# A routed mixture of experts on one core: the next expert's transposes go inside the prepared sequences, and the common tile gets its own PSUM bank

## The chip, the cores and the metric

The kernel runs on one core of a Trainium2 chip. The metric is the device time of one execution in microseconds (us); lower is better. Three runs of the kernel before gave 756.47, 759.58 and 760.03 us, so its median is 759.58 us.

## What is computed

Two blocks follow each other. The first is an attention over 4 batches x 8 heads x 768 positions x 64 columns, in which a position sees the 8 first keys and a window of 96. Its output, as 3072 rows of 512 numbers, goes into a block of 8 experts; each row goes through exactly one of them, the one with the highest cosine similarity. Everything is float32.

```python
expert_idx = np.argmax(logits, axis=1)
gate_w = probs[np.arange(N), expert_idx]
for e in range(E):
    mask = expert_idx == e
    h = np.maximum(x[mask] @ w1[e], 0.0)              # 512 -> 1024
    out[mask] = gate_w[mask, None] * (h @ w2[e])      # 1024 -> 512
```

How many rows an expert gets is known only when the program runs.

## The kernel before

**Attention.** It comes first, writes the 3072 rows to `x_dram`, and writes for each row a slot in `meta` (row number and gate) that is sorted by expert. The change leaves this part as it is.

**Experts.** The eight experts run one after the other, in Python's order of the loop `for e in range(n.E)` (line 840). On TensorE, ScalarE, VectorE and GpSimd the order of the instructions is the order in which the code is written (`manual_schedule`, line 836). Each expert has these steps:

- `load_rows` (line 629): SyncE loads 512 slots of `meta` into `emt`, VectorE casts the row numbers into `ids`, and GpSimd issues four indirect DMAs that gather 4 x 128 rows of `x_dram` into four tiles `xg`. It is written one expert ahead: expert e+1's rows are gathered at the start of expert e.
- `load_weights` (line 133): two DMAs of 2 MB each, into one of two sets of buffers in turn.
- `turn_rows` (line 651): the four tiles `xg` are transposed on TensorE, each with four transposes into one PSUM bank from the pool `work` (L657); VectorE copies each bank into `xT` (L658). In the tables below these are the "transposes" and the "copies".
- the first product (L690): 64 matmuls of `w1` with `xT`, only as wide as the expert has rows, rounded up to a multiple of 32. ScalarE puts the result through a relu into `hT` (L692), GpSimd clears what is left of the last 128 columns (L694).
- the second product, `second` (line 662): for each 128 rows a tile of 16 matmuls with `w2` into a bank of `work` (L668), VectorE multiplies it with the gate into `y` (L671), and GpSimd scatters `y` to the output with an indirect DMA (L672).

**Prepared sequences.** Because the width is known only at run time, the program holds 13 versions ("arms") of an expert's first product and of the tiles j = 1, 2, 3 of its second product, for the widths 128, 160, ... 512. Each engine jumps into the arm that fits (`tc.Switch`, line 682) and at its end jumps to the common code behind all arms. The common code of expert e holds a hint for the next jump (`switch_hint`, line 833), the transposes and copies of expert e+1 (`turn`, called as `between`, line 698), and the tile j = 0 of expert e's second product, which every width needs. The pool `work` has four banks for all of these, and `big` has two buffers of two banks for the first product.

In this data the eight experts take the widths 416, 320, 512, 320, 352, 384, 480 and 384. An arm of width 320, 352 or 384 has two tiles of the second product (j = 1, 2), one of 416, 480 or 512 has three. "The join" below is the stretch from the last matmul in an arm to the first matmul of the next expert's arm; there are seven of them.

Of the kernel before, what the change touches and what calls it, by code (L numbers as in the profile page):

```python
# [9 lines left out]
F32 = mybir.dt.float32  # L10
# [4 lines left out]
PSUM = bass.MemoryType.PSUM  # L15
# [3 lines left out]
P = 128  # L19
NEG = 1e9  # L20
CAP = 512
# [626 lines left out]
    return mt, ids, xgs  # L648


def turn_rows(k, rows):

    xT = k.xtp.tile([P, k.NC, CAP], F32, name="xT", tag="xT")
    for j, xg in enumerate(rows[2]):
        ps = k.work.tile([P, k.NC, P], F32, name="work", tag="work")
        for c in range(k.NC):
            k.nc.tensor.transpose(ps[:, c, :], xg[:, c * P : (c + 1) * P], k.ident[:])  # L657
        k.nc.vector.tensor_copy(out=xT[:, :, j * P : (j + 1) * P], in_=ps[:])  # L658
    return xT


def second(k, rows, hT, w2, j):

    nc = k.nc
    mt, ids, _ = rows
    ps = k.work.tile([P, k.DM], F32, name="work", tag="work")
    for f in range(k.NF):
        nc.tensor.matmul(ps[:], lhsT=hT[:, f, j * P : (j + 1) * P], rhs=w2[:, f, :],  # L668
                         start=f == 0, stop=f == k.NF - 1)
    y = k.yp.tile([P, k.DM], F32, name="y", tag="y")  # L670
    nc.vector.tensor_scalar_mul(y[:], ps[:], mt[:, j, 1:2])  # L671
    nc.gpsimd.indirect_dma_start(  # L672
        out=k.out[:, :], out_offset=bass.IndirectOffsetOnAxis(ap=ids[:, j : j + 1], axis=0),
        in_=y[:], in_offset=None, bounds_check=k.N - 1, oob_is_err=False,
    )


def expert(k, rows, xT, w1, w2, width=None, between=None):

    nc, tc = k.nc, k.tc  # L680
    hT = k.hp.tile([P, k.NF, CAP], F32, name="hT", tag="hT")
    arms = [len(WIDTHS) - 1] if width is None else tc.Switch(width.index, len(WIDTHS), hint=width.hint)
    for arm in arms:
        w = WIDTHS[arm]
        for f2 in range(k.NF // 2):
# [6 lines left out]
            nc.scalar.activation(hT[:, 2 * f2 : 2 * f2 + 2, 0:w], ps[:, :, 0:w], AF.Relu)  # L692
            if w % P:
                nc.gpsimd.memset(hT[:, 2 * f2 : 2 * f2 + 2, w : -(-w // P) * P], 0.0)  # L694
        for j in range(1, -(-w // P)):
            second(k, rows, hT, w2, j)
    if between:
        between()
    second(k, rows, hT, w2, 0)


# [18 lines left out]
def leftover(k):  # L720
# [18 lines left out]
    with tc.If(any_ > 0):  # L739
# [7 lines left out]
        with ExitStack() as inner:  # L747
# [10 lines left out]
            with tc.For_i(0, E * passes, 1) as i:  # L758
# [3 lines left out]
                with tc.If(n > 0):  # L762
# [2 lines left out]
                    nc.sync.dma_start(w1[:], k.w1[bass.ds(e, 1)].rearrange("o (c p) f -> p (o c) f", p=P))  # L765
                    nc.sync.dma_start(w2[:], k.w2[bass.ds(e, 1)].rearrange("o (f p) m -> p (o f) m", p=P))
                    rows = load_rows(k, k.meta[bass.ds(e * k.N + j * CAP, CAP), :])
                    expert(k, rows, turn_rows(k, rows), w1, w2)


def expert_pools(k, ctx):
# [8 lines left out]
def kernel(  # L780
# [13 lines left out]
    n = Net()  # L794
# [21 lines left out]
    with ExitStack() as moe:  # L816
# [2 lines left out]
        with ExitStack() as inner:  # L819
            window_attention(n, inner)  # L820

        n.work = ctx.enter_context(tc.tile_pool(name="work", bufs=4, space=PSUM))
        n.big = ctx.enter_context(tc.tile_pool(name="big", bufs=2, space=PSUM))
        wp_b = moe.enter_context(tc.tile_pool(name="wp_b", bufs=1))
        expert_pools(n, moe)
        choose_widths(n)
        next_ = Net()

        def prepare(e):
            next_.rows = load_rows(n, n.meta[e * n.N : e * n.N + CAP, :])  # L830

        def turn(e):
            tc.switch_hint(n.widths[e].index, len(WIDTHS), n.widths[e].hint)
            next_.xT = turn_rows(n, next_.rows)

        with tc.manual_schedule(engines=set(ARMS)):
            prepare(0)
            turn(0)
            w = n.w[0]
            for e in range(n.E):  # L840
                now, next_ = next_, Net()
                now.w = w
                if e + 1 < n.E:
                    prepare(e + 1)
                    w = new_weights(n, (wp_a, wp_b)[(e + 1) % 2])
                    load_weights(n, e + 1, w)
                expert(n, now.rows, now.xT, *now.w, n.widths[e], (lambda: turn(e + 1)) if e + 1 < n.E else None)
    n.scatters = None
    leftover(n)

# [27 lines left out]
```

## Time and profile before

| what | value |
|---|---|
| median of three runs | 759.58 us (756.47 to 760.03) |
| the profiled execution's own time | 746.06 us |
| span of the profiled execution | 744.3 us |
| TensorE busy | 629.3 us, 85% of the span |
| VectorE, ScalarE, GpSimd busy | 24%, 19%, 15% |
| attention, to the first matmul of the experts | about 0 to 284.8 us |
| experts, to the last matmul | 284.8 to 728.7 us |

The profile comes from one execution. Its page gives the busy time of each engine, a picture of the span in 40 slices, and the chain of work that ended last. The trace behind it gives each instruction with the idle time before it and what ended that idle time (`<-`). PE is TensorE's matmul side, DVE is VectorE, POOL is GpSimd, SPq is the DMA queue of SyncE. [...] "issue" is idle time in which an engine waited for nothing that the trace shows.

### The profile page before, as it was taken

How to read it: one execution, taken by the hardware profiler on the slowest of the kernel's cores; microseconds unless marked ns; L12 is line 12 of the kernel's file. 1: busy time of each engine (PE TensorE's matmuls, PEld its weight loads, DVE VectorE, ACT ScalarE, POOL GpSimd, SP SyncE). 2: the span in 40 equal slices, each digit the busy share in tenths (PEclk: the TensorE clock that was granted, in tenths of full speed). 3: DMA queues.
4: the chain of work that ended last, by engine and by line, in shares of the span. 5: the costliest groups of instructions: out<-in, count | busy, mean ns of one | idle time of the engine just before them, and what ended most of it. 6: DMA issues, size and time to landing. Idle time of an engine off the chain costs nothing.

```text
span 744.3 us, 8702 instructions
## 1 busy us (share of the span) xinstructions
PE 629.3 (85%) x3314; PEld 347.4 (47%) x3314; DVE 179.3 (24%) x509; ACT 141.0 (19%) x280; POOL 111.2 (15%) x146
## 2 busy tenths in 40 slices
PE   4889989989999408978969997979969969997991
PEld 2556655556566304534634443634535534443540
DVE  2434563564467511011020002011020020011000
ACT  3444543544453200100100100100100100100100
POOL 3110013013003232011112010211112012010010
PEclk9999999998899657997988998997988989997997
DMA  9856676840012942022434103532334134000000
GB/s 223 196 125 185 164 229 56 154 116 15 30 44 26 234 85 88 2 89 101 145 137 140 46 30 130 186 118 82 127 138 143 47 142 177 11 30 14 16 29 20
DMA packets 102683, 75.67 MB, mean 102 GB/s; under 512 B 83440, under 2 KB 83568, under 8 KB 102522
## 3 DMA queue, kind: packets, MB, share of 16 engines
q1 hardware_dynamic: 93610, 58.44, 29.5%
q0 software_dynamic: 5488, 14.71, 5.4%
q8 instruction: 51, 0.84, 0.5%
q10 hardware_dynamic: 3424, 0.79, 0.5%
q14 instruction: 110, 0.90, 0.4%
HBM read 61.11 MB, written 13.59 MB: 100 GB/s over the span
## 4 chain that ended last, share of the span: by engine, by line
PE 77%; DMA 7%; DVE 6%; issue 4%; ACT 2%; POOL 1%; DVEq 1%; another core or an unknown queue 0%; SPq 0%; ACTq 0%; POOLq 0%
PE work L668 27%; PE big L690 23%; PE sp L340 7%; PE od L370 6%; PE tp L323 3%; PE od L376 3%; PE work L657 3%; DMA x_dram<-xs 3%; DVE xT L658 3%; DVE ex L350 1%; DMA w2t<-in_moe_w_dram 1%; PE tp L433 1%; PE tp L408 1%; PE tp L411 1%; DMA meta<-mt,slot 1%
## 5 line engine op out<-in xcount | busy, mean ns | idle before, releaser
L668 PE MATMUL work<-w2t,hT 128*128 128x512 f32 x432 | 203.3, 631 | 5.5 <-DVE xT L658 5.5
L690 PE MATMUL big<-xT,w1t 128*128 128x320 f32 (+5 forms) x512 | 173.9, 501 | 0.9 <-DVE ids L639 0.9
L668 PEld LDWEIGHTS work<-w2t,hT 128*128 128x128 f32 x432 | 87.1, 204 | 115.8 <-issue 106.4
L690 PEld LDWEIGHTS big<-xT,w1t 128*128 128x128 f32 x512 | 98.3, 192 | 76.5 <-issue 42.4
L671 DVE TENSOR_SCALAR y<-work,emt 128x512 f32<-128x512 f32 x27 | 20.3, 751 | 360.8 <-PE work L668 360.8
L692 ACT ACTIVATE hT<-big 128x640 f32<-128x640 f32 (+5 forms) x32 | 26.6, 830 | 422.9 <-PE big L690 422.9
L350 DVE TENSOR_TENSOR ex<-ex,table 126x384 f32<-126x384 f32 (+1 forms) x128 | 67.4, 564 | 82.4 <-ACT ex L344 81.2
L672 POOL DMA_INDIRECT out_dram<-y,ids x27 | 26.8, 993 | 372.9 <-DVE y L671 240.8
L657 PE MATMUL work<-ident,xg 128*128 128x128 f32 x128 | 30.8, 386 | 57.7 <-DVE xT L658 38.3
L340 PE MATMUL sp<-qT,kT 64*126 64x192 f32 (+1 forms) x512 | 67.4, 366 | 6.1 <-ACT qT L328 5.1
L370 PE MATMUL od<-ex,v 126*64 126x192 f32 (+1 forms) x576 | 61.8, 322 | 5.3 <-POOL mt L200 3.8
L344 ACT ACTIVATE ex<-sp 126x768 f32<-126x768 f32 x64 | 49.1, 767 | 75.7 <-PE sp L340 68.2
L340 PEld LDWEIGHTS sp<-qT,kT 64*126 64x126 f32 x512 | 44.0, 197 | 26.7 <-issue 15.5
L657 PEld LDWEIGHTS work<-ident,xg 128*128 128x128 f32 x128 | 20.5, 193 | 69.6 <-DVE xT L658 45.2
L370 PEld LDWEIGHTS od<-ex,v 126*64 126x64 f32 x576 | 34.4, 140 | 24.3 <-issue 13.6
L376 PE MATMUL od<-ex,ones 126*32 126x192 f32 (+1 forms) x576 | 36.2, 321 | 0.0
L658 DVE COPY xT<-work 128x512 f32<-128x512 f32 x32 | 22.1, 692 | 51.7 <-PE work L657 32.0
L643 POOL DMA_INDIRECT xg<-x_dram,ids x32 | 30.9, 966 | 22.7 <-DVE ids L639 13.6
L202 POOL DMA_INDIRECT meta<-mt,slot x24 | 24.4, 1019 | 39.1 <-DVE slot L193 20.6
L323 PE MATMUL tp<-ident,k 128*128 128x128 f32 x96 | 19.9, 330 | 5.7 <-DMA k<-in_k_dram 5.5
L314 POOL COPY v<-v 30x1792 f32<-30x1792 f32 x8 | 13.7, 1714 | 65.4 <-DMA v<-in_v_dram 65.2
L323 PE MATMUL tp<-ident,q 128*128 128x128 f32 x96 | 19.9, 326 | 1.5 <-ACT kT L325 1.5
(117 smaller groups left out, 295.0 us busy)
## 6 DMA issues: line engine op xcount, KB each, us to landing
w1t<-in_moe_w_dram SPq DMA_DIRECT2D x8, 2048.0 KB, 8.9
w2t<-in_moe_w_dram SPq DMA_DIRECT2D x8, 2048.0 KB, 12.0
k<-in_k_dram SPq DMA_DIRECT2D x32, 192.0 KB, 3.3
v<-in_v_dram SPq DMA_DIRECT2D x32, 192.0 KB, 3.7
x_dram<-xs SPq DMA_DIRECT2D x24, 256.0 KB, 3.2
q<-in_q_dram SPq DMA_DIRECT2D x28, 192.0 KB, 3.4
q<-in_q_dram ACTq DMA_DIRECT2D x4, 192.0 KB, 5.4
xg<-x_dram,ids POOLq DMA_INDIRECT x32, 6.8
```

Of the source, the lines that this page charges most:

```text
L323: nc.tensor.transpose(ps[:, r * P : (r + 1) * P], src[:, 3 * half + r, :, :], k.ident[:])
L340: nc.tensor.matmul(sp[0:ROWS, e, a * n : (a + 1) * n], lhsT=t.kT[rows, j, 0:ROWS], rhs=t.qT[rows, j * BLK : j * BLK + n], start=True, stop ...
L344: nc.scalar.activation(ex, sp[0:ROWS, :, 0 : 2 * n], AF.Exp, scale=k.scale)
L350: nc.vector.tensor_tensor(out=exv, in0=exv, in1=tb, op=ALU.mult)
L370: nc.tensor.matmul(od[a][e * D : (e + 1) * D, cols], lhsT=g.v[0:ROWS, 2 * a + e, j, :], rhs=ex[:, e, a * n + c0 : a * n + c1], start=first ...
L376: nc.tensor.matmul(od[2][32 * i : 32 * i + 32, cols], lhsT=k.ones[0:ROWS, 0:32], rhs=ex[:, e, a * n + c0 : a * n + c1], start=first, stop= ...
L643: nc.gpsimd.indirect_dma_start(out=xg[:], out_offset=None, in_=k.x_dram[:], in_offset=bass.IndirectOffsetOnAxis(ap=ids[:, j : j + 1], axis=0),
L657: k.nc.tensor.transpose(ps[:, c, :], xg[:, c * P : (c + 1) * P], k.ident[:])
L658: k.nc.vector.tensor_copy(out=xT[:, :, j * P : (j + 1) * P], in_=ps[:])
L668: nc.tensor.matmul(ps[:], lhsT=hT[:, f, j * P : (j + 1) * P], rhs=w2[:, f, :], start=f == 0, stop=f == k.NF - 1)
L672: nc.gpsimd.indirect_dma_start(out=k.out[:, :], out_offset=bass.IndirectOffsetOnAxis(ap=ids[:, j : j + 1], axis=0), in_=y[:], in_offset=No ...
L690: nc.tensor.matmul(ps[:, i, 0:w], lhsT=w1[:, c, f * P : (f + 1) * P], rhs=xT[:, c, 0:w], start=c == 0, stop=c == k.NC - 1)
```

## The change

Four things change, all in the experts' part:

- `turn_rows` for expert e+1 is now called inside each of the 13 arms, behind the first product and ahead of the tiles j >= 1 of the second product. Its output tile `xT` is allocated ahead of the switch, in `expert`.
- The common code behind the arms holds only the hint for the next jump and the tile j = 0.
- The pool `work` has three banks instead of four; the fourth is the pool `work0`, which only the tile j = 0 uses.
- The names around it are put in order (`coming` instead of `between`, `next_` and `turn`); the gathers and the weights' loads are issued in the same order as before.

```diff
-def turn_rows(k, rows):
-
-    xT = k.xtp.tile([P, k.NC, CAP], F32, name="xT", tag="xT")
+def turn_rows(k, rows, xT):
+
     for j, xg in enumerate(rows[2]):
         ps = k.work.tile([P, k.NC, P], F32, name="work", tag="work")
...
-    ps = k.work.tile([P, k.DM], F32, name="work", tag="work")
+    ps = k.work0.tile([P, k.DM], F32, name="work0") if j == 0 else k.work.tile([P, k.DM], F32, name="work", tag="work")
...
+def hint(k, width):
+    k.tc.switch_hint(width.index, len(WIDTHS), width.hint)
...
-def expert(k, rows, xT, w1, w2, width=None, between=None):
+def expert(k, rows, xT, w1, w2, width=None, coming=None):
 
     nc, tc = k.nc, k.tc
     hT = k.hp.tile([P, k.NF, CAP], F32, name="hT", tag="hT")
+    if coming:
+        coming.xT = k.xtp.tile([P, k.NC, CAP], F32, name="xT", tag="xT")
     arms = [len(WIDTHS) - 1] if width is None else tc.Switch(width.index, len(WIDTHS), hint=width.hint)
     for arm in arms:
         w = WIDTHS[arm]
...
+        if coming:
+            turn_rows(k, coming.rows, coming.xT)
         for j in range(1, -(-w // P)):
             second(k, rows, hT, w2, j)
-    if between:
-        between()
+    if coming:
+        hint(k, coming.width)
     second(k, rows, hT, w2, 0)
...
-        n.work = ctx.enter_context(tc.tile_pool(name="work", bufs=4, space=PSUM))
+        n.work = ctx.enter_context(tc.tile_pool(name="work", bufs=3, space=PSUM))
+        n.work0 = ctx.enter_context(tc.tile_pool(name="work0", bufs=1, space=PSUM))
```

TensorE before, the common code behind the arms of the third expert (width 512), with the semaphores that each row waits for; DVE is VectorE's, DMASW a gather's, DMAHW a weight load's:

```order
L833 SWITCH_STRIDE
L833 ISA
L833 BRANCH_PREFETCH_HINT
L657 MATMUL work<-ident,xg 128x128 [waits DMASW4_49,DVE_49]
L657 MATMUL work<-ident,xg 128x128 x3
L657 MATMUL work<-ident,xg 128x128 [waits DMASW5_49,DVE_49]
L657 MATMUL work<-ident,xg 128x128 x3
L657 MATMUL work<-ident,xg 128x128 [waits DMASW6_49,DVE_49]
L657 MATMUL work<-ident,xg 128x128 x3
L657 MATMUL work<-ident,xg 128x128 [waits DMASW7_49,DVE_49]
L657 MATMUL work<-ident,xg 128x128 x3
L668 MATMUL work<-w2t,hT 128x512 [waits DMAHW6_49,DVE_49]
```

The hint, the four groups of transposes and then the tile j = 0 follow each other behind the arms, and each of the five banks is asked for with a wait for VectorE.

TensorE now, inside the 512-wide arm of the same expert, from the last quarter of the first product:

```order
L694 MATMUL big<-xT,w1t 128x512 x7
L656 MATMUL work<-ident,xg 128x128 [waits DMASW4_49]
L656 MATMUL work<-ident,xg 128x128 x3
L656 MATMUL work<-ident,xg 128x128 [waits DMASW5_49]
L656 MATMUL work<-ident,xg 128x128 x3
L656 MATMUL work<-ident,xg 128x128 [waits DMASW6_49]
L656 MATMUL work<-ident,xg 128x128 x3
L656 MATMUL work<-ident,xg 128x128 [waits DMASW7_49,DVE_49]
L656 MATMUL work<-ident,xg 128x128 x3
L666 MATMUL work<-w2t,hT 128x512 [waits DMAHW6_49,DVE_49]
L666 MATMUL work<-w2t,hT 128x512 x3
```

The transposes stand ahead of the tile j = 1; three groups wait for their gather alone, the fourth and the tile j = 1 also for VectorE.

TensorE now, the common code behind the arms of that expert:

```order
L879 UNCONDITIONAL_BRANCH
L677 SWITCH_STRIDE
L677 ISA
L677 BRANCH_PREFETCH_HINT
L666 MATMUL work_6851<-w2t,hT 128x512 [waits DMAHW6_49]
L666 MATMUL work_6851<-w2t,hT 128x512 x3
L666 MATMUL work_6851<-w2t,hT 128x512 [waits Activation_49]
```

The tile j = 0, now in its own bank, stands directly behind the hint and doesn't wait for VectorE any more. VectorE's copies moved in the same way, from the common code to the head of each arm's VectorE part, ahead of the `y` of the tiles j >= 1. ScalarE's, GpSimd's and SyncE's rows stand as they stood.

## Rows read from the trace of the kernel before

**Rows 1.** The page: the span, and TensorE's busy time.

```profile
span 744.3 us, 8702 instructions
PE 629.3 (85%) x3314; PEld 347.4 (47%) x3314; DVE 179.3 (24%) x509; ACT 141.0 (19%) x280; POOL 111.2 (15%) x146
```

**Rows 2.** Timeline of TensorE: start, us, instructions, [idle before <- what ended it].

```profile
309.53 20.76 PE L668 MATMUL work<-w2t,hT 128*128 128x512 f32 x48
330.13 0.60 PE L657 MATMUL work<-ident,xg 128*128 128x128 f32 x4
334.73 1.12 PE L657 MATMUL work<-ident,xg 128*128 128x128 f32 x4 [4.00 <-DVE xT L658]
336.63 1.12 PE L657 MATMUL work<-ident,xg 128*128 128x128 f32 x4 [0.78 <-DVE xT L658]
...
340.43 8.92 PE L668 MATMUL work<-w2t,hT 128*128 128x512 f32 x16 [0.78 <-DVE xT L658]
349.19 17.39 PE L690 MATMUL big<-xT,w1t 128*128 128x320 f32 x64
...
448.18 0.60 PE L657 MATMUL work<-ident,xg 128*128 128x128 f32 x4
450.49 0.66 PE L657 MATMUL work<-ident,xg 128*128 128x128 f32 x4 [1.70 <-DVE xT L658]
451.93 0.66 PE L657 MATMUL work<-ident,xg 128*128 128x128 f32 x4 [0.79 <-DVE xT L658]
453.37 1.12 PE L657 MATMUL work<-ident,xg 128*128 128x128 f32 x4 [0.78 <-DVE xT L658]
455.27 9.52 PE L668 MATMUL work<-w2t,hT 128*128 128x512 f32 x16 [0.78 <-DVE xT L658]
```

**Rows 3.** Windows: the seven joins and one arm; busy us per engine, PEclk, DMA, GB/s.

```profile
330.13:349.19 19.06, 12.71 (x34) 6.33 (x33) 3.52 (x5) 0.00 (x0) 0.98 (x1) 0.73 0.33 117
349.19:380.14 30.95, 30.95 (x97) 18.19 (x96) 1.58 (x3) 2.81 (x4) 6.51 (x10) 1.00 0.35 121
380.14:400.12 19.98, 12.97 (x34) 6.45 (x33) 3.52 (x5) 0.00 (x0) 0.99 (x1) 0.74 0.32 114
...
448.18:464.63 16.45, 12.39 (x34) 6.02 (x33) 3.52 (x5) 0.00 (x0) 0.98 (x1) 0.79 0.42 147
...
495.59:515.60 20.01, 13.19 (x34) 6.28 (x32) 3.52 (x5) 0.00 (x0) 0.99 (x1) 0.74 0.33 115
...
548.26:567.47 19.21, 12.87 (x33) 6.45 (x32) 3.52 (x5) 0.00 (x0) 0.99 (x1) 0.73 0.35 120
...
601.84:621.82 19.98, 13.13 (x34) 6.49 (x32) 3.52 (x5) 0.00 (x0) 0.99 (x1) 0.74 0.34 121
...
668.18:687.18 19.00, 12.62 (x34) 6.30 (x33) 3.52 (x5) 0.00 (x0) 0.98 (x1) 0.73 0.04 14
```

**Rows 4.** Timeline of VectorE around the first and the third join.

```profile
330.33 0.75 DVE L671 TENSOR_SCALAR y<-work,emt 128x512 f32<-128x512 f32 x1 [6.12 <-PE work L668]
333.99 0.69 DVE L658 COPY xT<-work 128x512 f32<-128x512 f32 x1 [2.90 <-issue]
...
449.74 0.69 DVE L658 COPY xT<-work 128x512 f32<-128x512 f32 x1 [0.61 <-issue]
451.18 0.69 DVE L658 COPY xT<-work 128x512 f32<-128x512 f32 x1 [0.75 <-PE work L657]
```

**Rows 5.** Timeline of GpSimd: first and last of the four gathers at an expert's start.

```profile
351.70 1.00 POOL L643 DMA_INDIRECT xg<-x_dram,ids x1 [0.30 <-issue]
...
355.55 0.95 POOL L643 DMA_INDIRECT xg<-x_dram,ids x1 [0.30 <-issue]
```

**Rows 6.** The page's DMA issues of the weights: count, KB each, median us to landing.

```profile
w1t<-in_moe_w_dram SPq DMA_DIRECT2D x8, 2048.0 KB, 8.9
w2t<-in_moe_w_dram SPq DMA_DIRECT2D x8, 2048.0 KB, 12.0
```

**Rows 7.** The tile `xg`: time of the 32 gathers from issue to landing.

```profile
DMA to landing us min/median/max: 3.7/6.8/7.4
```

More of the change, by code (lines that the diff above doesn't have):

```diff
@@ L658, in turn_rows @@
         k.nc.vector.tensor_copy(out=xT[:, :, j * P : (j + 1) * P], in_=ps[:])
-    return xT
 def second(k, rows, hT, w2, j):
@@ L767, in leftover @@
                     rows = load_rows(k, k.meta[bass.ds(e * k.N + j * CAP, CAP), :])
-                    expert(k, rows, turn_rows(k, rows), w1, w2)
+                    xT = k.xtp.tile([P, k.NC, CAP], F32, name="xT", tag="xT")
+                    turn_rows(k, rows, xT)
+                    expert(k, rows, xT, w1, w2)
 def expert_pools(k, ctx):
@@ L826 @@
         choose_widths(n)
-        next_ = Net()
         def prepare(e):
[L830 to L834, printed above, removed]
+            t = Net()
+            t.width = n.widths[e]
+            t.rows = load_rows(n, n.meta[e * n.N : e * n.N + CAP, :])
+            t.w = n.w[0]
+            if e > 0:
+                t.w = new_weights(n, (wp_a, wp_b)[e % 2])
+                load_weights(n, e, t.w)
+            return t
         with tc.manual_schedule(engines=set(ARMS)):
-            prepare(0)
-            turn(0)
-            w = n.w[0]
+            coming = prepare(0)
+            hint(n, coming.width)
+            coming.xT = n.xtp.tile([P, n.NC, CAP], F32, name="xT", tag="xT")
+            turn_rows(n, coming.rows, coming.xT)
             for e in range(n.E):
[L841 to L847, printed above, removed]
+                now, coming = coming, prepare(e + 1) if e + 1 < n.E else None
+                expert(n, now.rows, now.xT, *now.w, now.width, coming)
     n.scatters = None
```

## The prediction, made before the change was run

> **What bounds the kernel now.** I read the page first, then TensorE's timeline over the experts, then windows cut at the points that the timeline shows, and last what VectorE and GpSimd do there. The page says that TensorE is busy for 85% of the 744.3 us and no other engine for more than 24% [rows 1], so the question is what TensorE waits for and at which clock it runs. Inside an arm there is nothing to win: TensorE is busy for all of 30.95 us, and its clock is 1.00 [rows 3]. A tile of the second product takes a third of the 20.60 us from 309.53 to 330.13, so 6.87 us [rows 2].
>
> The joins are different. In the first one [rows 2] four transposes run directly behind the arm, in 0.60 us; then TensorE waits 4.00 us for VectorE, and each further group waits 0.78 us for the copy of the group before it, though the pool has four banks. After the waits the groups take 1.12 us instead of 0.60, and the tile j = 0 takes 8.92 us instead of 6.87. The windows show why: the granted clock of a join is 0.73 to 0.79 [rows 3], so it falls to the lower level within it and rises again only during the tile j = 0. The long wait has its cause on VectorE [rows 4]: after the arm's last `y` it waits for nothing that the trace shows, 2.90 us, before the first copy. In the third join, whose arm is the last of the thirteen and lies next to the common code, that is 0.61 us. So it is the price of VectorE's jump out of the arm. TensorE pays no such price at the same place: its 0.60 us group follows the arm without idle time.
>
> The seven joins take 19.06, 19.98, 16.45, 20.01, 19.21, 19.98 and 19.00 us [rows 3], together 133.7 us. That is the stretch that the change touches.
>
> **The change, part by part.** *Removed from the joins:* all that stands in them except the tile j = 0. That tile names no wait for VectorE now, and it has its own bank. TensorE reaches the common code as early as now (the 0.60 us group shows that), with 16 matmuls to run instead of four transposes and a wait. So I expect no idle time and, since the arm before it ran at 1.00, the upper clock: 6.87 us. The floor is 6.87, the other end is what it takes now, 8.92 to 9.52 us [rows 2]; I take the floor, because the same 16 matmuls behind dense ones take it in every arm.
>
> *Added to the arms:* 16 transposes per expert. Behind dense work a group of four takes 0.60 us [rows 2], four of them 2.4 us. The copies could hold them up. By the third join [rows 2, 4] a copy starts 0.69 us after its group (451.18 against 450.49) and lasts 0.69 us. With three banks the fourth group needs the first copy, done at 1.38 us, before it would start at 1.8; the tile j = 1 needs the second copy, done at about 2.1 us, and comes at 2.4. So the copies stay just covered. Bounds: 2.1 us (only the copy of the second group counts) and, if each group waited for the copy before it, four times the 1.44 us from 450.49 to 451.93, 5.8 us [rows 2]. I take 2.4, since the order names a wait for VectorE at the fourth group only; the relu of the last quarter of the first product gets these 2.4 us as extra cover.
>
> *Moved:* four copies per expert on VectorE, to the head of its arm. It enters the arm while TensorE is in the first product, at least 17 us long [rows 2], so a jump of 2.90 us is hidden. Its jump out of the arm stays, but now only the `y` of the tile j = 0 comes after it, and that is due 6.87 us later: the cover is 4 us. *GpSimd* has the same rows. Its gathers for the next expert still start at the start of an expert, but are needed sooner. The last one is issued 6.4 us after the first product's start at 349.19 [rows 2, 5] and lands at most 7.4 us later [rows 7], so at 13.8 us; the shortest first product ends at 17.4. Covered by 3.6 us. *SyncE:* the load of `w1` is freed at the arm's end and that of `w2` at the join's, so the two now lie about 7 us apart instead of 19. With 8.9 and 12.0 us to landing [rows 6] they overlap by some 2 us, and have a whole expert's time before they are needed: nothing. *Fewer banks, the hint, the renaming:* nothing by themselves; the hint comes about 6.9 us ahead of the next jump instead of 16 to 20.
>
> *The sum.* Before 133.7 us; after 7 x (2.4 + 6.87) = 64.9 us; gain 68.8 us. The span would be 675.5 us, and the profiled execution's own 746.06 us would become 677.3. That execution lies 13.5 us below the median of the runs, 759.58, and nothing on the page says where those 13.5 us are. I take the gain off the median: 759.58 - 68.8 = 690.8, **691 us**. If the change also took what makes the runs slower than the profiled execution, it would be 677, and that is my low end.
>
> [...] Groups of transposes at the upper clock take 0.60 and 0.66 us; in the third join the second and third group still do, and only the fourth, 5.2 us after the arm's end, takes 1.12 [rows 2]. From these rows 2.4 us of transposes between dense matmuls leave the clock where it is. [...]
>
> **The rivals.**
> *The clock falls in the arms.* Seven times a stretch like the present tile j = 0, with 8.92 to 9.52 us instead of 6.87 [rows 2]: 2.1 to 2.7 us each, so 14 to 19 us, and 705 to 709 in all. For it: the joins show that the clock falls and what it costs [rows 3]. Against it: in the third join 1.9 us of transposes and 3.3 us of waits pass before the first group at the lower clock, at 453.37 [rows 2]. Chance 0.12.
>
> *TensorE's jump into the next arm is no longer hidden.* The hint now stands 6.9 us ahead, and the arms have grown by 16 transposes. If a jump costs TensorE what it costs VectorE beyond the near case, 2.90 - 0.61 = 2.3 us [rows 4], seven make 16 us: 707. Against it: TensorE leaves the arm now without a gap, with instructions queued ahead. [...] Chance 0.10.
>
> *The three banks don't rotate,* as the four don't now, and each group waits for the copy before it. Then 5.8 instead of 2.4 us per expert, 24 us: 715, and with the clock falling behind it up to 19 us more. Against it: the order names no wait for VectorE at the second and third group. Chance 0.03.
>
> *Slower than before: the gathers come late.* TensorE takes its work in order, so a late gather now holds up the whole second product, which at present runs ahead of it. The place is the first group of transposes in an arm; two loads of 2 MB are now closer to the gathers. For landing in L us instead of 7.4, six experts (the first one's gathers are early) lose L + 6.4 less the length of their first products. Those take 17.39 us at width 320 [rows 2], so 21.4 at their mean width of 395, and the loss is 6 x (L - 15.0). That eats the 68.8 us at L = 26.5; at L = 30 the time is 759.6 - 68.8 + 90 = 781. Against it: the gathers land in 3.7 to 7.4 us beside a load of `w2` already [rows 6, 7]. Chance 0.02.
>
> **How the numbers follow.** Forecast 0.73, the rivals 0.12, 0.10, 0.03 and 0.02. The range runs from 677 (above) to 709, which takes in the clock rival and most of the jump rival and leaves out some 0.12. About 0.5%, or 4 us, is what a measurement of this kernel can tell from no change; every case but the late gathers lies far below 755, so faster 0.97, slower 0.02, and 0.01 for a loss that just cancels.
>
> **What would show it.** In the profile after: joins of about 6.9 us with a tile j = 0 and nothing else; PEclk 1.00 in them and in the arms; four groups of about 0.6 us between first and second product, 2.1 to 2.4 us in all, with no idle time that VectorE's copies end; VectorE's idle time of about 3 us at the arm's end still there, now ahead of the last `y`; no idle time of TensorE at the first matmul of an arm. A granted clock under 1.00 in the arms would show the first rival, "issue" at an arm's head the second, waits of 0.8 us between the groups the third, and waits for `xg` the last. I am wrong if the joins shorten as said and the time still stays above 709: then something outside TensorE's row set the end.

## The result, and the profile after

The change takes 687.87 us (median of 4 runs, 682.62 to 689.28) against 758.03 us for the kernel before (4 runs, 748.6 to 760.03): 70.2 us less, a ratio of 0.91 with a 95% interval of 0.8996 to 0.9203. The forecast was 691 us, the range 677 to 709.

The page of the changed kernel, to be held against [rows 1]: span, busy time, the granted clock of TensorE over 40 slices (PEclk, a 9 for 90% of full speed or more), and three groups.

```profile
span 685.8 us, 8692 instructions
...
PE 605.1 (88%) x3314; PEld 338.0 (49%) x3314; DVE 178.6 (26%) x509; ACT 141.9 (21%) x280; POOL 110.6 (16%) x146
...
PEclk9999998979899996579999999999999999999996
...
L666 PE MATMUL work<-w2t,hT 128*128 128x512 f32 x432 | 187.4, 594 | 0.0
...
L657 DVE COPY xT<-work 128x512 f32<-128x512 f32 x32 | 20.2, 684 | 157.9 <-PE work L656 157.9
```

From the second expert on the clock has no slice under 9 until the last one. The 432 matmuls of the second product have 0.0 us of idle time ahead of them, and no copy waits for "issue" any more.

TensorE's timeline over the first three experts of the changed kernel (start, duration, engine and line, idle time before it):

```profile
297.61 24.51 PE L694 MATMUL big<-xT,w1t 128*128 128x416 f32 x64 [0.79 <-DVE xT L657]
321.96 2.04 PE L656 MATMUL work<-ident,xg 128*128 128x128 f32 x16
323.94 27.73 PE L666 MATMUL work<-w2t,hT 128*128 128x512 f32 x64
351.51 17.39 PE L694 MATMUL big<-xT,w1t 128*128 128x320 f32 x64
368.74 2.10 PE L656 MATMUL work<-ident,xg 128*128 128x128 f32 x16
370.78 20.87 PE L666 MATMUL work<-w2t,hT 128*128 128x512 f32 x48
391.48 27.63 PE L694 MATMUL big<-xT,w1t 128*128 128x512 f32 x64
```

An expert took seven such rows before (most of the first one's stand in [rows 2]) and takes three here, and behind the first of these rows there isn't one idle time. The tiles of the second product are one row of 64 or 48 matmuls, the tile j = 0 its last 16.

Windows of the changed kernel: the first expert's transposes, its three tiles in the arm, its join, the second expert's first product, its transposes (busy time of each engine, then PEclk as a share of full speed, DMA share, GB/s):

```profile
321.96:323.94 1.98, 1.98 (x17) 1.65 (x16) 1.34 (x3) 0.87 (x1) 0.00 (x0) 1.00 0.02 4
323.94:344.64 20.70, 20.70 (x49) 9.23 (x49) 2.64 (x4) 0.00 (x0) 2.03 (x2) 1.00 0.37 129
344.64:351.51 6.87, 6.87 (x17) 3.04 (x16) 0.75 (x1) 0.00 (x0) 0.98 (x1) 1.00 0.06 19
351.51:368.74 17.23, 17.23 (x66) 12.11 (x64) 0.83 (x2) 2.11 (x3) 5.50 (x9) 1.00 0.58 200
368.74:370.78 2.04, 2.04 (x18) 1.66 (x16) 1.35 (x3) 0.71 (x1) 0.00 (x0) 1.00 0.01 4
```

The join is 6.87 us long where it was 19.06 [rows 3], and PEclk is 1.00 in every window, the transposes among them.

VectorE in the changed kernel, from the first expert's transposes to its join, to be held against [rows 4]:

```profile
322.60 2.48 DVE L657 COPY xT<-work 128x512 f32<-128x512 f32 x4 [24.97 <-PE work L656]
331.11 0.75 DVE L669 TENSOR_SCALAR y<-work,emt 128x512 f32<-128x512 f32 x1 [6.03 <-PE work L666]
...
344.85 0.75 DVE L669 TENSOR_SCALAR y<-work,emt 128x512 f32<-128x512 f32 x1 [6.12 <-PE work L666]
351.71 0.75 DVE L669 TENSOR_SCALAR y<-work,emt 128x512 f32<-128x512 f32 x1 [6.12 <-PE work L666]
```

VectorE's jump lies between the last two rows: its branch starts at 344.9 us, its next instruction, the hint in the common code, at 347.9. Both `y` waited the same 6.12 us for TensorE, so nothing of these 3.0 us is left to see in them.

**Where the time went.** From the first expert's first matmul to the end of the last tile ("the experts part" below) the kernel before takes 728.42 - 284.82 = 443.6 us, the changed one 670.11 - 297.61 = 372.5: 71.1 us less. The two profiled executions' own times, 746.06 and 687.63, differ by only 58.4 us, because the changed one reached its first expert 12.8 us later, at 297.61 instead of 284.82. The profiled execution of e1 below is a slow one (699.82 us): it reaches its first expert only at 303.68 us, while its matmuls behind that take as long as in the others.

### The profile page after: what moved, and what is told of

Its sections match the earlier page's. It is cut to its first block, busy times and chain, and to the rows that moved or that the text cites. A ratio compares the mean times of both kernels' runs of the same rounds, so it can differ in the third digit from the quotient of the medians.

```text
span 685.8 us, 8692 instructions
## 1 busy us (share of the span) xinstructions
PE 605.1 (88%) x3314; PEld 338.0 (49%) x3314; DVE 178.6 (26%) x509; ACT 141.9 (21%) x280; POOL 110.6 (16%) x146
## 4 chain that ended last, share of the span: by engine, by line
PE 56%; DMA 3%; DVE 1%; POOL 1%; issue 0%; ACT 0%; POOLq 0%; SPq 0%; ACTq 0%
PE work L666 27%; PE big L694 25%; PE work L656 2%; DMA x_dram<-xs 1%; DMA meta<-mt,slot 1%; DMA xg<-x_dram,ids 1%; DMA emt<-meta 0%; POOL xg L643 0%; PE tp L433 0%; PE tp L408 0%; PE tp L411 0%; PE od L370 0%; POOL out_dram L670 0%; PE od L376 0%; DVE y L669 0%
## 5 line engine op out<-in xcount | busy, mean ns | idle before, releaser
L666 PE MATMUL work<-w2t,hT 128*128 128x512 f32 x432 | 187.4, 594 | 0.0
L666 PEld LDWEIGHTS work<-w2t,hT 128*128 128x128 f32 x432 | 81.5, 190 | 101.0 <-issue 99.5
L350 DVE TENSOR_TENSOR ex<-ex,table 126x384 f32<-126x384 f32 (+1 forms) x128 | 68.8, 575 | 91.9 <-ACT ex L344 83.8
L370 PE MATMUL od<-ex,v 126*64 126x192 f32 (+1 forms) x576 | 63.6, 325 | 7.6 <-POOL mt L200 3.8
L657 DVE COPY xT<-work 128x512 f32<-128x512 f32 x32 | 20.2, 684 | 157.9 <-PE work L656 157.9
L656 PE MATMUL work<-ident,xg 128*128 128x128 f32 x128 | 19.0, 295 | 20.7 <-DMA xg<-x_dram,ids 20.7
L656 PEld LDWEIGHTS work<-ident,xg 128*128 128x128 f32 x128 | 15.4, 151 | 25.6 <-DMA xg<-x_dram,ids 21.1
L433 PE MATMUL tp<-ident,xd 128*128 128x128 f32 x96 | 16.4, 299 | 8.8 <-DVE lh L423 8.3
```

The source lines that it names most:

```text
L350: nc.vector.tensor_tensor(out=exv, in0=exv, in1=tb, op=ALU.mult)
L370: nc.tensor.matmul(od[a][e * D : (e + 1) * D, cols], lhsT=g.v[0:ROWS, 2 * a + e, j, :], rhs=ex[:, e, a * n + c0 : a * n + c1], start=first ...
```

## The experiments

Each time stands beside runs of the kernel before on the same chip: e1 to e4 beside 760.43 us, e5 to e7 beside 761.03, e8 to e11 beside 749.33, e12 beside 760.88. The experts part comes from the profiled execution.

| kernel | median us | ratio to before, 95% | experts part us |
|---|---|---|---|
| the change | 687.87 | 0.91 (0.8996 to 0.9203) | 372.5 |
| e1 one pool of four banks | 692.37 | 0.9091 (0.9028 to 0.9155) | 378.5 |
| e2 own bank alone | 716.66 | 0.9434 (0.9374 to 0.9494) | 400.4 |
| e3 transposes at the arm's end | 716.46 | 0.9449 (0.9383 to 0.9515) | 402.9 |
| e4 transposes behind tile j = 0 | 690.53 | 0.9111 (0.9042 to 0.918) | 379.7 |
| e5 before, copies on ScalarE | 719.41 | 0.9439 (0.9332 to 0.9546) | 407.3 |
| e6 transposes twice | 706.40 | 0.931 (0.9241 to 0.9378) | 388.9 |
| e7 no hint | 686.74 | 0.9033 (0.8964 to 0.9102) | 372.2 |
| e8 ahead of the arm's last tile | 681.02 | 0.9095 (0.9046 to 0.9145) | 375.3 |
| e9 twice, at the arm's end | 739.29 | 0.9885 (0.982 to 0.995) | 434.2 |
| e10 second weights later | 676.97 | 0.9054 (0.9016 to 0.9092) | 373.1 |
| e11 the change again | 678.61 | 0.9058 (0.9007 to 0.9109) | 372.8 |
| e12 as e9, loads turned round | 750.74 | 0.9876 (0.9818 to 0.9934) | 434.1 |

**e1: the change without the common tile's own bank.**

```diff
-    ps = k.work0.tile([P, k.DM], F32, name="work0") if j == 0 else k.work.tile([P, k.DM], F32, name="work", tag="work")
+    ps = k.work.tile([P, k.DM], F32, name="work", tag="work")
...
-        n.work = ctx.enter_context(tc.tile_pool(name="work", bufs=3, space=PSUM))
-        n.work0 = ctx.enter_context(tc.tile_pool(name="work0", bufs=1, space=PSUM))
+        n.work = ctx.enter_context(tc.tile_pool(name="work", bufs=4, space=PSUM))
```

> The transposes stay inside the arms, but the tile j = 0 takes its bank from the shared pool of four again. Theory (the own bank frees the common tile from the arm's last multiplication on VectorE, no more): the tile j = 0 waits once per join for the arm's last y, 0.2 us until it starts and 0.75 us for itself, so about 1.0 us; seven joins of 7.9 us instead of 6.9, clock still 1.00, about 695 us. Rival (the own bank is what frees it from VectorE's jump out of the arm): joins of 4 us more with a lower clock, 720 us or above. If the bank is worth nothing: 688.

TensorE's timeline of e1, the first join:

```profile
352.22 7.13 PE L666 MATMUL work<-w2t,hT 128*128 128x512 f32 x16 [0.84 <-DVE y L669]
```

The tile j = 0 now waits for the `y` of the arm's last tile, 0.84 us. With that the experts part is 6.0 us longer than the change's, 0.9 us per join; so moving the transposes, without the bank, brings 65.1 of the 71.1 us. That wait is for the `y`, not for VectorE's jump: the jump comes after that `y`. The medians' ratios, 0.9091 and 0.91, don't tell the two apart.

**e2: the bank alone, transposes left where they were.** The kernel before, with these lines:

```diff
-    ps = k.work.tile([P, k.DM], F32, name="work", tag="work")
+    ps = k.work0.tile([P, k.DM], F32, name="work0") if j == 0 else k.work.tile([P, k.DM], F32, name="work", tag="work")
...
-        n.work = ctx.enter_context(tc.tile_pool(name="work", bufs=4, space=PSUM))
+        n.work = ctx.enter_context(tc.tile_pool(name="work", bufs=3, space=PSUM))
+        n.work0 = ctx.enter_context(tc.tile_pool(name="work0", bufs=1, space=PSUM))
```

> The kernel before, with its transposes behind the arms, and only the pool split into three banks and one for the tile j = 0. Theory (the waits in the joins are VectorE's jump plus a chain through one bank): the chain breaks up, the jump stays. The first group waits about 1 us for the arm's last y, the second and third follow at once, the fourth waits for the first copy, which comes 2.9 us after that y, and j = 0 follows it at about 5 us: joins of 12 to 13 us instead of 19, about 712 us. Rival (the move alone matters): no change, 758. Rival (the banks are all of it): 690.

TensorE's timeline of e2, the first join and the matmuls behind it:

```profile
345.98 1.53 PE L657 MATMUL work<-ident,xg 128*128 128x128 f32 x12 [0.85 <-DVE y L671]
349.93 0.66 PE L657 MATMUL work<-ident,xg 128*128 128x128 f32 x4 [2.42 <-DVE xT L658]
350.43 7.03 PE L668 MATMUL work<-w2t,hT 128*128 128x512 f32 x16
357.30 17.39 PE L690 MATMUL big<-xT,w1t 128*128 128x320 f32 x64
```

VectorE in the same join of e2:

```profile
345.17 0.75 DVE L671 TENSOR_SCALAR y<-work,emt 128x512 f32<-128x512 f32 x1 [6.11 <-PE work L668]
349.19 2.48 DVE L658 COPY xT<-work 128x512 f32<-128x512 f32 x4 [3.27 <-issue]
```

Three groups run in a row, and only the fourth waits for a copy. The jump of 3.27 us is still there, and 2.42 us of it reach TensorE, but the waits of 0.78 us between the groups [rows 2] are gone, and this join's last tile is back at 7.03 us from 8.92 (in four of the seven joins it still takes 8.39 to 8.73). So the bank alone brings 43.2 of the 71.1 us. Why the pool of four made each group wait for the copy before it, and the pool of three does not, no run here shows. Four banks as such don't do it: in e1, with the pool of four, the 16 transposes in an arm run without a wait, in a row of 1.91 us.

**e3: the transposes at the end of the arm, behind its tiles j >= 1.**

```diff
-        if coming:
-            turn_rows(k, coming.rows, coming.xT)
         for j in range(1, -(-w // P)):
             second(k, rows, hT, w2, j)
+        if coming:
+            turn_rows(k, coming.rows, coming.xT)
```

> The change, but the transposes stand at the end of each arm, behind the tiles j >= 1, not between the two products. Theory (it matters only that the copies come before VectorE's jump and that the jump is covered by the tile j = 0): the four groups take 2.0 to 2.5 us there too, the joins 6.9 us, the clock 1.00; 688 to 691 us. Rival (the place between the products matters, since it covers the last relu, or the copies at the arm's end delay the jump until it shows): more than 1 us per expert, 696 us or more, with idle time ahead of j = 1 or of the next first product.

A clear miss: 716.46 us. TensorE's timeline of e3, the joins of the first two experts (three and two tiles in the arm):

```profile
318.07 20.76 PE L666 MATMUL work<-w2t,hT 128*128 128x512 f32 x48
338.67 2.26 PE L656 MATMUL work<-ident,xg 128*128 128x128 f32 x16
347.15 10.19 PE L666 MATMUL work<-w2t,hT 128*128 128x512 f32 x16 [6.21 <-issue]
...
388.14 2.26 PE L656 MATMUL work<-ident,xg 128*128 128x128 f32 x16
390.67 7.12 PE L666 MATMUL work<-w2t,hT 128*128 128x512 f32 x16 [0.28 <-issue]
398.45 27.70 PE L694 MATMUL big<-xT,w1t 128*128 128x512 f32 x64 [0.66 <-issue]
```

TensorE waits 6.21 us for nothing that its timeline shows, just where it leaves the arm; the two other arms with three tiles have 6.58 and 4.02 us, the four with two tiles 0.27 to 0.34. After each long stop the tile j = 0 takes 8.96 to 10.19 us instead of 6.87; after the first of them PEclk is 0.69 (347.15 to 357.18). The trace also has TensorE's branches (under the name PEldq; times in ns, then the start). Here are those out of the first and out of the second arm:

```profile
L879 PEldq COMPARE_BRANCH  x1: 6183/6183/6183, 340.3 to 340.3; - x1
L879 PEldq COMPARE_BRANCH  x1: 318/318/318, 389.7 to 389.7; - x1
```

The branch itself lasts 6.18 us in the first, 6.54 and 4.05 us out of the two other arms with three tiles, and 0.32 us out of the four with two. So the long stops are TensorE's jump out of the arm. In the kernel before, the same branch takes 0.29 to 0.31 us out of all seven arms. In the changed one it takes 3.01, 2.22 and 0.39 us out of those with three tiles, without any idle time: in the first of them it begins 7.7 us before the arm's last matmul ends, behind tiles of 6.87 us each, while here it begins 0.65 us before the end, behind 16 short transposes of 2.26 us in all. e8 and e9 test this. The jump into the next arm takes 3.79 to 7.18 us in e3; the tile j = 0 hides it but for 0.66 and 0.34 us, at the heads of two arms.

**e4: the transposes out of the arm again, but behind the tile j = 0** (the change's pools).

```diff
-        if coming:
-            turn_rows(k, coming.rows, coming.xT)
         for j in range(1, -(-w // P)):
             second(k, rows, hT, w2, j)
     if coming:
         hint(k, coming.width)
     second(k, rows, hT, w2, 0)
+    if coming:
+        turn_rows(k, coming.rows, coming.xT)
```

> The transposes stay out of the arms, behind the tile j = 0 instead of ahead of it, with the split pool. Theory (VectorE's jump is the cost, and the tile j = 0 can cover it): the jump is over when j = 0 ends; then three groups run at once, the fourth waits for the first copy, and the next first product waits for the last copy: joins of 6.9 + 3 to 4 us, clock near 1.00, so 1 to 2 us per join over the change with its 2.0 us of transposes: 695 to 703 us. Rival (the transposes have to be in the prepared sequences): joins near those of before, 740 us or more.

TensorE's timeline of e4, the end of the first join:

```profile
316.42 27.63 PE L666 MATMUL work<-w2t,hT 128*128 128x512 f32 x64
343.88 2.26 PE L656 MATMUL work<-ident,xg 128*128 128x128 f32 x16
346.73 17.46 PE L694 MATMUL big<-xT,w1t 128*128 128x320 f32 x64 [0.59 <-DVE xT L657]
```

690.53 us: nearly the whole gain without a transpose in an arm. The tile j = 0 covers VectorE's jump as well as the arm does: its `y` at 344.09 us waited 6.11 us for TensorE, the ones in the arm 6.12. What is left is the wait of the next first product for the last copy, 0.58 to 1.14 us at each of the seven joins; with transposes that take 2.26 instead of 2.04 us, that is most of the 7.2 us by which the experts part is longer than the change's.

**e5: the kernel before, with the copies on ScalarE.**

```diff
-        k.nc.vector.tensor_copy(out=xT[:, :, j * P : (j + 1) * P], in_=ps[:])
+        k.nc.scalar.copy(out=xT[:, :, j * P : (j + 1) * P], in_=ps[:])
```

> The kernel before, with the copies of the transposes on ScalarE instead of VectorE. ScalarE has left the arm after the last relu, long before the join. Theory (the 4.0 us wait at the first copy is VectorE's jump out of the arm): the first copy starts within about 0.2 us of its group, the long wait falls from 4.0 to about 0.9 us, the chain through one bank stays at some 1.5 us per group, and the clock falls less: joins of 13 to 15 us instead of 19, about 715 to 730 us. Rival (the wait is in TensorE's own jump or in the bank): the first wait stays at about 4 us, 755 us or more.

TensorE's timeline of e5, the first join:

```profile
338.06 0.60 PE L657 MATMUL work<-ident,xg 128*128 128x128 f32 x4
339.33 0.66 PE L657 MATMUL work<-ident,xg 128*128 128x128 f32 x4 [0.68 <-ACT xT L658]
340.67 0.66 PE L657 MATMUL work<-ident,xg 128*128 128x128 f32 x4 [0.68 <-ACT xT L658]
...
343.33 7.13 PE L668 MATMUL work<-w2t,hT 128*128 128x512 f32 x16 [0.67 <-ACT xT L658]
```

ScalarE has nothing to do at an arm's end and reaches the common code early: in the kernel before its branch out of the first arm starts at 309.7 us and its first instruction behind it at 312.3, while TensorE leaves that arm at 330.13. The wait of 4.00 us [rows 2] becomes 0.68, and PEclk in this join is 1.00 (338.06 to 350.30); in the fifth the tile j = 0 takes 7.13 us too, in the other five still 8.68 to 9.72. So the 4.00 us were VectorE's lateness, not the transposes or the gathers. The chain of one wait per group stays, 0.67 to 0.73 us each.

**e6: the transposes twice in each arm** (the second time over the first).

```diff
         if coming:
             turn_rows(k, coming.rows, coming.xT)
+            turn_rows(k, coming.rows, coming.xT)
```

> The change with the transposes and copies done twice in each arm (the second time over the first). Theory (transposes between dense matmuls leave the clock at the upper level and cost 2.0 us for four groups, held by copies of 0.6 us each): 4.2 to 4.6 us instead of 2.0 per expert, seven times 2.2 to 2.6, so 15 to 18 us: 703 to 706 us, clock 1.00. Rival (transposes let the clock fall): clock under 1.00 behind them, and 1 to 3 us more per expert, 712 to 725 us.

Windows of e6: the first expert's 32 transposes, then its four tiles of the second product:

```profile
318.52:322.90 4.38, 4.38 (x34) 3.34 (x32) 3.74 (x7) 0.87 (x1) 0.00 (x0) 1.00 0.04 10
322.90:350.47 27.57, 27.57 (x66) 12.26 (x66) 3.39 (x5) 0.00 (x0) 3.00 (x3) 1.00 0.28 100
```

Twice the transposes cost 4.38 us instead of 1.98, the clock is 1.00 in them and behind them, and the experts part grows by 16.4 us, which is seven times 2.3. The rival of the falling clock is out, up to twice the transposes that the change has.

**e7: the change without the hint in the common code** (the one ahead of the first expert stays).

```diff
-    if coming:
-        hint(k, coming.width)
     second(k, rows, hT, w2, 0)
```

> The change without the hint for the next jump in the common code. Theory (TensorE's instructions are queued ahead of it, so its jump into an arm is hidden like its jump out): no idle time at an arm's head, 688 us. Rival (the hint, now only 6.9 us ahead, is what hides the jump): at least VectorE's 2.3 us of idle time at the head of each of seven arms, 704 us or more, and a lower clock if it lasts.

No difference: 372.2 us for the experts part against 372.5, and no idle time at the head of an arm. The hint is worth no time here. TensorE's branch into an arm takes 3.27 to 3.76 us in all seven cases without it, against 3.28 to 3.68 in four and 0.4 in three with it in the profile of the change, and the tile j = 0 of 6.87 us hides either.

**e8: the transposes in the arm, ahead of its last tile.**

```diff
-        if coming:
+        last = -(-w // P) - 1
+        for j in range(1, last + 1):
+            if coming and j == last:
+                turn_rows(k, coming.rows, coming.xT)
+            second(k, rows, hT, w2, j)
+        if coming and last == 0:
             turn_rows(k, coming.rows, coming.xT)
-        for j in range(1, -(-w // P)):
-            second(k, rows, hT, w2, j)
```

> The change, but the transposes stand ahead of the last tile of each arm: between the first product's end and its place in the run before last one or two tiles lie ahead of them, and one tile of 16 long matmuls behind them. Theory (at the arm's end the 16 short transposes left too little queued work to cover TensorE's own jump, 2.5 us in the arms with two tiles and 6.3 to 8.8 us in those with three): one tile of 6.87 us plus the tail of the transposes covers the short jump and nearly all of the long one, so idle time behind the arms of 0 with two tiles and 0 to 2 us with three; about 688 to 692 us. Rival (any place but the one directly behind the first product costs the time): idle time of 4 us and more behind the wide arms, 710 us or above.

TensorE's timeline of e8, the first expert's last tile in the arm and the tile j = 0:

```profile
328.19 7.11 PE L666 MATMUL work<-w2t,hT 128*128 128x512 f32 x16
335.77 7.13 PE L666 MATMUL work<-w2t,hT 128*128 128x512 f32 x16 [0.48 <-issue]
```

With one tile of 6.87 us ahead of the jump the stop out of the three arms with three tiles shrinks from 6.21, 6.58 and 4.02 us to 0.48, 0.36 and 0; the arms with two have none. The branch itself is as long as in e3 (6.90, 6.73 and 3.71 us). Long matmuls ahead of the jump hide it, as the reading of e3 says. The experts part is 27.6 us shorter than in e3, and still 2.8 longer than with the transposes ahead of all tiles.

**e9: e3 with the transposes twice, so with 32 more instructions in each arm.**

```diff
         if coming:
             turn_rows(k, coming.rows, coming.xT)
+            turn_rows(k, coming.rows, coming.xT)
```

> The transposes at the arm's end, as in the run that cost 28 us, but done twice, so every arm has 16 transposes more. Theory (the long jumps come with the arm's length in instructions, and the arms with two tiles now are as long as those with three were): idle time behind the arms with two tiles rises from 0.3 to some 2 to 4 us, although more work is queued; behind those with three it stays at 2 to 4 us; 720 to 735 us. Rival (something else about the wide arms, or their distance): two-tile arms stay at 0.3 us or less, and three-tile arms fall by the 2.2 us that is queued more; about 720 us.

TensorE's timeline of e9, the first two joins:

```profile
329.47 4.65 PE L656 MATMUL work<-ident,xg 128*128 128x128 f32 x32
337.33 10.18 PE L666 MATMUL work<-w2t,hT 128*128 128x512 f32 x16 [3.21 <-issue]
...
378.31 4.65 PE L656 MATMUL work<-ident,xg 128*128 128x128 f32 x32
387.69 8.82 PE L666 MATMUL work<-w2t,hT 128*128 128x512 f32 x16 [4.74 <-issue]
```

739.29 us, more than the expectation had. Two things moved in opposite directions. Out of the arms with three tiles the stop is shorter than in e3 (3.21, 3.92 and 0.90 us, each about 3 us less). It isn't that the 2.4 us of further transposes hide more: the branch begins 0.65 us before the last transpose ends in both, and is itself shorter. Out of those with two tiles, which now have as many instructions as the arms with three had in e3 (128 matmuls and as many weight loads), it is 4.74 to 6.24 us instead of 0.3. Two readings offer themselves: the long jump goes with how much an arm holds, or with a load of 2 MB that is under way at the jump. Windows of e9 over three of these stretches, from the first transpose to the tile j = 0 (the last but one column is the DMA share):

```profile
329.47:337.33 7.86, 4.65 (x34) 3.32 (x32) 5.53 (x9) 0.00 (x0) 0.98 (x1) 0.96 0.75 274
378.31:387.69 9.38, 4.65 (x33) 3.31 (x32) 5.53 (x9) 0.00 (x0) 1.00 (x1) 1.00 0.65 240
...
664.49:670.04 5.55, 4.65 (x34) 3.32 (x32) 5.35 (x9) 0.00 (x0) 0.98 (x1) 1.00 0.11 38
```

The last of them, out of the seventh expert's arm with three tiles, has no load of weights beside it, and its stop is the shortest, 2.3 and 3.0 us less than the two others out of such arms; in e3 it is 2.2 and 2.6 us less (4.02 against 6.21 and 6.58).

**e12: e9 with the loads turned round,** to have none under way at the jump.

```diff
+    if e > 1:
+        nc.sync.dma_start(w[1][:], k.w2[e].rearrange("(f p) m -> p f m", p=P))
     nc.sync.dma_start(w[0][:], k.w1[e].rearrange("(c p) f -> p c f", p=P))
-    nc.sync.dma_start(w[1][:], k.w2[e].rearrange("(f p) m -> p f m", p=P))
+    if e <= 1:
+        nc.sync.dma_start(w[1][:], k.w2[e].rearrange("(f p) m -> p f m", p=P))
```

> e9 with the load of w2 issued ahead of that of w1 from the third expert on. The load of w2 waits for the end of the tile j = 0, so no 2 MB load is under way while TensorE leaves an arm. Theory A (a load under way lengthens the jump, and the arm's size does too): the stops out of the arms with three tiles, 3.21, 3.92 and 0.90 us in e9, become about 0.9 in all three, like the last one, which has no load beside it in e9 either; those out of the arms with two tiles, 4.74 to 6.24 us, fall by 2 to 3 us but stay at 2 to 4; the experts part falls from 434.2 us to about 415 (six stops shorter by 2 to 3 us, and shorter stretches at the lower clock behind them), the median to some 718 to 725 us. Theory B (the load alone makes the long jumps out of the arms with two tiles): those stops fall to 0.3 us or less, the experts part to about 395 to 403. Theory C (the load has no part in it): stops as in e9, experts part 434.

The edit didn't do what it says. SyncE isn't among the engines whose order is that of the code, and its queue still has `w1` first, as its timeline of e12 shows:

```profile
337.78 0.37 SPq L137 DMA_DIRECT2D w1t<-in_moe_w_dram  x1
354.13 0.37 SPq L136 DMA_DIRECT2D w2t<-in_moe_w_dram  x1
```

So e12 is e9 once more (434.1 us for the experts part, against 434.2; stops of 3.24, 4.05 and 0.92 us out of the arms with three tiles, 4.97 to 6.28 out of the others) and tells nothing of the three theories. What makes the jump long stays open, but TensorE's branches in the traces kept so far narrow it down (three tiles: first, third and seventh expert):

| kernel | matmuls in an arm, two / three tiles | branch out, two tiles, us | branch out, three tiles, us |
|---|---|---|---|
| before | 96 / 112 | 0.29 to 0.31 | 0.30, 0.30, 0.31 |
| the change | 112 / 128 | 0.30 to 0.31 | 3.01, 2.22, 0.39 |
| e3 | 112 / 128 | 0.32 | 6.18, 6.54, 4.05 |
| e8 | 112 / 128 | 0.31 to 0.32 | 6.90, 6.73, 3.71 |
| e6 | 128 / 144 | 0.95 to 1.06 | 0.31, 0.31, 0.31 |
| e9 | 128 / 144 | 4.78 to 6.22 | 3.25, 3.96, 0.88 |

What an arm holds matters: out of arms of up to 112 matmuls the branch takes 0.29 to 0.32 us in all fourteen traces, and in e9 it takes 4.78 us and more out of those that grew from 112 to 128. Its length alone doesn't set it: the arms of e6 and e9 hold the same instructions in another order. A load of 2 MB isn't enough: in e3 it is issued 1.4 us before the branch out of the arms with two tiles too (388.33 against 389.75), and that takes 0.32 us. A load may lengthen a long jump: out of the seventh expert's arm, which has none beside it, the branch is 1.8 to 3.2 us shorter than out of the two others in the change, e3, e8 and e9; no run separates that from the arm itself.

**e10 and e11: the second expert's weights later, and the change once more.** The changed kernel's first expert starts 12.8 us later than that of the kernel before. One theory was that the loads of the second expert's weights crowd the first gathers; in e10 they wait for the last of these.

```diff
+    if e == 1:
+        for i in (i1, i2):
+            k.tc.add_manual_dep(i.ins, k.first_gather.ins.name,
...
```

> The change, with the two loads of the second expert's weights held back until the first expert's gathers have landed. They now lie in the hand-over, beside the last writes of the attention's rows. Theory (the time left lies ahead of the experts: TensorE sits idle for 20 us there, and the last writes take 10 us to land beside 4 MB of weights, against 3 to 6 us at the median): the first expert starts 4 to 8 us earlier after the last routing step, the experts' part stays at 372.5 us, 680 to 684 us. Rival (the writes are slow for another reason): 688 us, no change; if the weights come too late for the second expert, an idle time at its first matmul.

> The changed kernel once more, unaltered, beside the run with the weights later. Theory (what differs between executions lies ahead of the experts): 683 to 690 us, the experts' part within 1 us of 372.5 and the start of the first expert's matmuls anywhere from 285 to 304 us. Rival (the experts' part varies as much): an experts' part that differs by more than 3 us.

No difference: 0.9054 and 0.9058. (Both medians lie below what was expected; on this chip the kernel before takes 749.33 us.) From the last matmul of the routing to the first of the experts there are 281.79 - 255.42 = 26.4 us in e10 and 290.49 - 263.33 = 27.2 in e11; in the kernel before it is 25.3, in the profile of the change 26.5. So this stretch isn't where the executions differ. They differ ahead of it: leaving e1 out, the first expert starts anywhere from 281.79 (e10) to 300.82 us (e7), the unaltered change at 297.61 and 290.49; the attention there is the same in all of them.

None of these versions is measurably faster than the change.

## Why the prediction was right, point by point

- **The joins.** "No idle time and the upper clock: 6.87 us" is what the profile shows, at PEclk 1.00. The tile j = 0 waits for no other engine, and 6.87 us of it hide VectorE's jump (3.0 us in the first join, from its branch to its next instruction).
- **The sum.** Predicted 68.8 us, measured 71.1 in the experts part and 70.2 between the medians. The term that was off is the transposes in the arms: 2.4 us predicted from four groups of 0.60, 1.98 to 2.05 measured from the first start to that of the next row, so about 0.5 per group where they follow each other without a wait. Seven times 0.4 us is the 2.3 that were missing, and a bit more.
- **The parts of the gain.** The prediction gave one sum for the joins and didn't say which edit earns what. The runs do: 443.6 us before, 400.4 with the bank alone (e2), 379.7 with the transposes also behind the tile j = 0 (e4), 372.5 with them in the arm. That is 43.2, 20.7 and 7.2 us, in this order of the edits; in the other order the move brings 65.1 us and the bank 6.0 on top of it (e1), so each alone brings more than half. Once the bank is split, being inside the arms and not behind the tile j = 0 earns the least, and that step shows in the traces alone; the medians' ratios of e4 and of the change have overlapping intervals.
- **The clock.** From groups of 0.60 and 0.66 us I concluded that 2.4 us of transposes between dense matmuls leave the clock where it is. The traces bear that out: 16 transposes in 1.98 us, 32 in 4.38 (e6), all at PEclk 1.00. In the first join of the kernel before, PEclk is 1.00 over the first four transposes (330.13 to 330.73), 0.89 over the wait of 4.00 us behind them, 0.50 from 334.73 to 344.00 and 0.99 from 344.00 to 346.00.
- **"TensorE pays no such price"** holds for the kernel before, where the branch out of an arm takes 0.29 to 0.31 us, and fails for the changed one, where it takes 3.01 and 2.22 us out of two of the three arms with three tiles. The prediction carried the reading over, although the arms had grown by 16 transposes. That the sum came out is luck at this point: the tiles behind the transposes happen to hide the jump. I gave the place between the two products a value as cover for the relu only. Its real worth is that long matmuls stand behind the transposes at the jump: the same change with the transposes at the arm's end loses 30.4 us of its 71.1 (e3).
- **VectorE's jump.** I expected its idle time of about 3 us to be seen ahead of the last `y`. It isn't: that row names TensorE, with the same 6.12 us as the rows before it, although 3.0 us pass from VectorE's branch (344.9) to its next instruction (347.9). Hidden behind the wait for TensorE, the jump leaves no idle time of its own.
- **The weights' loads.** I had `w1` freed at the arm's end and `w2` at the join's, 7 us apart. SyncE's timeline of the changed kernel:

```profile
331.11 0.37 SPq L135 DMA_DIRECT2D w1t<-in_moe_w_dram  x1
351.70 0.37 SPq L136 DMA_DIRECT2D w2t<-in_moe_w_dram  x1
...
370.87 0.37 SPq L135 DMA_DIRECT2D w1t<-in_moe_w_dram  x1
391.68 0.37 SPq L136 DMA_DIRECT2D w2t<-in_moe_w_dram  x1
```

  The first starts with the end of the tile j = 1 (three tiles) or of the transposes (two tiles), so they lie 20.6 and 20.8 us apart and don't overlap. The conclusion (it costs nothing) holds, the reason doesn't.
- **The 13.5 us.** I took the gain off the median and kept 677 as the low end, in case the change also took what sets the profiled execution apart. The runs speak against that: between executions of the changed kernel the difference lies ahead of the experts (e11). Of the kernel before there is one trace only, so for it this isn't shown.
- **The rivals.** Clock: out (windows, e6). TensorE's jump into the next arm: it exists, with up to 3.05 us in the kernel before and 0.39 to 3.68 in the change, but the tile j = 0 hides it, even without the hint (e7); its jump out of the arm was the one to think of. Banks that don't rotate: out, 16 transposes in one row. Late gathers: out, no matmul of the later experts waits for `xg`.

## What to carry to other kernels

Behind a jump, put first the work that waits for no other engine, and let it be long enough to cover the other engines' jumps (here 6.87 us over VectorE's 3.0); a hand-over to another engine belongs well away from the point where that engine jumps (here it cost TensorE a wait of 4.00 us). Ahead of a jump, leave long instructions queued: 16 transposes of 2.26 us left stops of up to 6.58 us (e3), a tile of 6.87 us at most 0.48 (e8). An engine that shows no idle time there may only have had enough work ahead of it, as in the change, where the branch takes up to 3.01 us without a stop. And look at a shared ring of buffers first: splitting off one bank, three lines, brought 43.2 of the 71.1 us with nothing else changed.

## What the runs showed that I had not expected

- TensorE's jump out of a prepared sequence: its branch takes 0.3 us in the kernel before, up to 3.0 in the changed one, and up to 6.9 where transposes stand near the arm's end (e8); why it grows is open. It leaves no idle time behind three tiles of 6.87 us (the change), at most 0.48 us behind one (e8), and up to 6.58 us behind 16 transposes (e3).
- A hint for the next jump that can be left out at no cost in time (e7).
- The start of the experts moves by up to 19 us between executions whose attention is the same (by 8.7 us on one chip, e8 to e11), more than the difference between several of these versions; the experts part, taken from the trace, repeats within 0.3 us for the change (372.5 and 372.8).
